# Loads split between GpSimd and SyncE, turns by DMA, and fixed orders in an attention and max-out kernel

## Chip, cores and metric

One core of a Trainium2 chip. The time is the device time of one execution in microseconds (us), measured over several runs; lower is better. Engines: TensorE (PE; its weight loads are PEld), VectorE (DVE), ScalarE (ACT), GpSimd (POOL), and SyncE (SP), which only issues transfers here. Transfers run on 16 DMA engines.

## What is computed

Attention over 4 batches, 8 heads, 768 positions and 64 channels, in which each query sees the keys less than 16 positions away and one summary (max for k, mean for v) per block of 32 positions; then a feed-forward stage over all 3072 rows of 512 channels.

```
k_sum = k.reshape(B, H, nb, 32, D).max(axis=3);  v_sum = v.reshape(B, H, nb, 32, D).mean(axis=3)
scores_l = scale * q @ k.T          (kept where |i - j| < 16)
scores_s = scale * q @ k_sum.T + log(32)
a = softmax(concat[scores_l, scores_s]);  x = a @ concat[v, v_sum]
g = maximum(x @ w1, x @ w2);  out = g @ w_out
```

All inputs and the output are float32; the matmuls run in bfloat16.

## The kernel before

The second stage is rewritten: with wd = w2 - w1, out = x (w1 w_out) + relu(x wd) w_out. The product w1 w_out (called w1o) is computed once.

Names in the plan: the first digit of a tag is the batch (0 to 3), the second the pair of heads (0 to 3), the third the group of queries (0 or 1: half of the positions, in three tiles of 128 rows). Loads: k and q per pair (k02 is batch 0, pair 2), v per half of the heads (v00, v01), a0 to a3 and b0 to b3 (quarters of w1 and w2), o0 to o3 (of w_out).

Per pair, `prep` casts k and q to bfloat16, turns each on PE by six 128x128 transposes (line 422), copies them from PSUM in the order of positions ("place"), takes the block maxima on DVE ("max"), copies the 32 neighbours of each tile of 64 positions ("halo") and the 24 block maxima into every tile ("sums"), so that one key tile holds 96 keys and the summaries. `scores` does 26 small matmuls per group (line 478), each on 64 rows for one head, then the exponential on ACT (line 485). In batch 0 the window is applied on PE by adding a tile of large negative numbers (line 470); in later batches by a multiplication on DVE or GpSimd (line 490). `values` does 12 matmuls per group (line 507) against a v that `place_v` has spread over tiles of 64 positions, with the block means (line 379) copied into each tile; DVE then divides (lines 518, 520) to x. After two pairs x is turned on PE by six transposes (line 536) and copied to xt.

`make_w12` makes wd and a bfloat16 w1, turns w1 on PE (line 573); `make_w1o` multiplies (line 594). `maxout` per batch and group: eight "hidden" tiles of four matmuls of 384 columns (line 607) with a relu each (line 612), then three "out" tiles, each in three parts of four matmuls of 512 columns: x w1o first (line 624), then two halves of g w_out (line 631); a copy and a store follow. Each part can stand apart in PE's order.

All loads and stores are issued by SP. 40 groups of four matmuls on the identity (line 666, "warm") occupy PE while it has nothing else. The order of each engine's work comes from a planner in the kernel: each step has a duration, dependences and a priority number, and whenever an engine is free in the planner's account the step with the best priority that can run is put next in that engine's program. The buffers (rings of tiles: six for float32 k and q, two for float32 v, eight banks of PSUM) are handed out in the same pass. On the chip each engine runs its program in that order and waits at the head of it.

Of the kernel before, what the change touches and what calls it, by code (L numbers as in the profile page):

```python
# [14 lines left out]
F32 = mybir.dt.float32  # L15
# [7 lines left out]
C = dict(  # L23
    first='k2 v0 k1 k0 q1 q0 b0 k3 q3 a0 v1 b2 b3 q2 a1 o0 a3 a2 o1 o2 b1 o3',
    later='q2 q0 k1 k3 k2 q3 q1 k0 v0 v1',
    b0=dict(v=84, vcast=('POOL ACT', 'ACT DVE'), vevac=('DVE', 'ACT'), pair=83,
             scores=(-128, 370), values=(-484, 84),
             kcast=('DVE POOL ACT', 'DVE POOL', 'ACT', 'DVE POOL ACT'),
             qcast=('DVE ACT', 'ACT', 'ACT POOL', 'POOL DVE'),
             kplace=('ACT', 'ACT', 'DVE ACT', 'DVE ACT'), qplace='ACT DVE',  # L30
             halo=('DVE POOL', 'DVE POOL', 'DVE POOL', 'POOL'),
             sums=('DVE POOL', 'DVE POOL', 'ACT', 'ACT'), mask='PE',
             xt=('DVE', 'DVE', 'DVE', 'ACT DVE')),
    b=dict(v=-315, vcast=('ACT DVE', 'ACT'), vevac='ACT', pair=95, scores=(43, 18),
             values=(-92, -34), kcast=('DVE POOL ACT', 'POOL', 'DVE POOL', 'DVE POOL'),
             qcast=('ACT POOL', 'DVE POOL ACT', 'DVE POOL ACT', 'POOL DVE'),
             kplace=('ACT', 'ACT', 'DVE', 'DVE'), qplace=('ACT', 'DVE', 'ACT', 'ACT DVE'),
             halo=('DVE ACT POOL', 'DVE ACT POOL', 'DVE ACT POOL', 'DVE ACT'),
             sums=('POOL', 'DVE', 'DVE POOL', 'POOL'), mask='DVE POOL', xt='DVE'),
    w12=2240, w1t=-1070, wo=1060, w1o=-830, moe=1300, wd='POOL',  # L40
    w1b=('ACT', 'POOL ACT', 'POOL ACT', 'POOL DVE'),
    wocast=('POOL DVE', 'POOL DVE', 'POOL DVE', 'DVE'), w1tcopy='ACT DVE', w1ocopy='ACT DVE',
    relu='ACT', outcopy='ACT', caps=dict(kq=5, sc=6, av=6, mm=7, x=3, warm=1), hold=2, warm=40,
    xdma=(), kqdma=(), tdma=1.5, hide=5.5, amean=8.5)
# [52 lines left out]
class Plan:  # L97
# [4 lines left out]

    LAG = {"PE": 0.25, "ACT": 0.2, "DVE": 0.15, "POOL": 0.2, "SP": 0.1}
    LAND, DEPTH, TURN = 2.2, 8, 0.08

    def __init__(self):
        self.tasks = []

    def op(self, engine, us, fn, read=(), write=(), change=(), touch=(), behind=(), prio=0.0, label="",
           mode="", port=False, dma=0.0, fill=False):  # L110
        t = Task()
        t.choice = isinstance(us, dict)
        t.us = us if t.choice else {engine: us}
        t.fn, t.label, t.mode, t.port, t.dma, t.fill = fn, label, mode, port, dma, fill
        t.prio = (prio, len(self.tasks))
        t.new, t.behind = [*write, *change], behind
        t.deps = {w for b in (*read, *change) for w in b.writers}
        for b in t.new:
            b.writers.append(t)
        for b in (*read, *touch, *t.new):  # L120
            b.users.append(t)
        self.tasks.append(t)
        return t
# [9 lines left out]

    def run(self):
        follow, left = {t: [] for t in self.tasks}, {}
        for t in self.tasks:
            left[t] = len(t.deps) + len(t.behind)
            for d in (*t.deps, *t.behind):
                follow[d].append(t)
        waiting = {e: [] for e in self.LAG}  # L140
        events = [0.0]

        def offer(t):
            t.at = max((d.done + self.LAG["SP" if d.dma else d.engine] for d in t.deps), default=0.0)
            heapq.heappush(events, t.at)
            for e in t.us:
                bisect.insort(waiting[e], t, key=lambda t: t.prio)

        for t in self.tasks:
            if not left[t]:  # L150
                offer(t)
        busy = dict.fromkeys(self.LAG, 0.0)
        landed = [0.0] * self.DEPTH
        order, mode = [], ""
        while len(order) < len(self.tasks):
            now = heapq.heappop(events)
            for e, queue in waiting.items():
                if busy[e] > now:
                    continue
                able = [t for t in queue if t.at <= now and not (t.dma and landed[-self.DEPTH] > now)]  # L160
                if e == "PE":
                    many = {m: sum(t.mode == m for t in able) > 1 for m in ("rows", "cols")}
                    able.sort(key=lambda t: t.fill or (t.mode != mode if mode else (
                        t.mode != "" and not many[t.mode] and now < t.at + C["hold"])))
                t = next((t for t in able if self.slots(t, now)), None)
                if t is None:
                    continue
                t.start, t.engine, us = now, e, t.us[e]
                if t.dma:
                    busy[e] = now + t.dma  # L170
                    t.done = max(landed[-1], now + self.LAND) + us
                    landed.append(t.done)
# [4 lines left out]
                elif e == "DVE" and t.port:  # L177
                    busy[e] = t.done = max(now, busy["POOL"]) + us
# [3 lines left out]
                for other in t.us:  # L182
# [540 lines left out]
```

## Time and profile before

| | |
|---|---|
| median of 3 runs | 181.82 us (179.27 to 182.73) |
| the profiled execution | 180.56 us, its span 178.9 us |
| granted TensorE clock | 0.995 |
| HBM read, written | 25.17 MB, 6.29 MB |

The busy share of an engine is an average over the whole span; the rows of single stretches tell which stage is limited by what. "Idle before" is the time an engine stood before a group, with what ended it. A row of the chain of waits names the work, or the transfer, that ended last at that point. DMA share can be over 1, since packets on one engine overlap. A few matmul records can be missing from a trace.

### The profile page before, as it was taken

Reading aid. Unit: us, or ns where it says so; the run is one execution under the profiler, and the core shown is the slowest. Engines: PE = TensorE matmul, PEld = TensorE weight load, DVE = VectorE, ACT = ScalarE, POOL = GpSimd, SP = SyncE. Lnnn points to the kernel's source line nnn. Section 1 sums busy time; section 2 is a strip of 40 time slices with the busy share of each in tenths; the row PEclk is TensorE's granted clock in tenths of the full one; section 3 lists DMA queues with packets and bytes.
Section 4 is the critical chain, followed back from the end, with each engine's and each line's share of the span. In section 5 each row is a group of like instructions: output and inputs, shape, how many; then the busy total and the mean of one; then the engine's idle time right before and its main releaser. Section 6 shows DMA issues by size and latency. Waiting matters only on the chain.

```text
span 178.9 us, 4689 instructions
## 1 busy us (share of the span) xinstructions
PE 167.5 (94%) x1946; PEld 102.3 (57%) x1968; DVE 100.7 (56%) x193; ACT 115.0 (64%) x188; POOL 57.6 (32%) x74
## 2 busy tenths in 40 slices
PE   6999878999999999989999999999999999999991
PEld 6976745665544666557545664664565545654440
DVE  4294984879799679879935770396772201200000
ACT  3597987578886882498989541896828238471212
POOL 7123436938373550037677500324110000000000
PEclk9999999999999999999999999999999999999998
DMA  5999999999979999999811101210111013000333
GB/s 149 280 376 332 295 385 388 402 382 238 290 222 276 299 256 349 260 251 312 279 59 62 59 4 59 87 36 0 60 62 62 0 59 117 4 0 0 117 117 117
DMA packets 42261, 31.76 MB, mean 178 GB/s; under 512 B 25856, under 2 KB 38144, under 8 KB 42240
## 3 DMA queue, kind: packets, MB, share of 16 engines
q1 hardware_dynamic: 42240, 31.46, 59.3%
q8 instruction: 15, 0.25, 0.6%
q14 instruction: 6, 0.05, 0.1%
HBM read 25.17 MB, written 6.29 MB: 176 GB/s over the span
## 4 chain that ended last, share of the span: by engine, by line
PE 70%; DMA 15%; issue 5%; DVE 4%; ACT 2%; SPq 1%; POOL 0%; POOLq 0%; DVEq 0%; ACTq 0%
PE banks L607 24%; PE banks L631 17%; PE banks L624 10%; DMA kqf<-in_q_dram 5%; DMA wf<-in_moe_w_out_dram 5%; DMA vf<-in_v_dram 4%; PE banks L478 3%; PE banks L507 3%; PE banks L422 3%; PE banks L594 3%; PE banks L666 3%; DVE kqb L277 2%; PE banks L536 2%; ACT vx L277 1%; PE banks L379 1%
## 5 line engine op out<-in xcount | busy, mean ns | idle before, releaser
L607 PE MATMUL banks<-xt,wd 128*128 128x384 bf16 x256 | 45.8, 327 | 0.0
L631 PE MATMUL banks<-wo,g 128*128 128x512 bf16 x181 | 44.7, 380 | 1.1 <-issue 0.8
L612 ACT ACTIVATE g<-banks 128x384 bf16<-128x384 f32 x64 | 31.3, 492 | 11.3 <-PE banks L607 10.8
L277 ACT COPY o<-banks 128x512 f32<-128x512 f32 x24 | 14.1, 585 | 31.8 <-PE banks L631 31.6
L607 PEld LDWEIGHTS <-wd 128*128 128x128 bf16 x256 | 23.6, 98 | 14.6
L485 ACT ACTIVATE pb<-banks,bias 128x768 bf16<-128x768 f32 x32 | 28.0, 900 | 3.4 <-PE banks L478 2.6
L631 PEld LDWEIGHTS <-g 128*128 128x128 bf16 x192 | 17.4, 98 | 18.2
L490 POOL TENSOR_TENSOR pb<-pb,mask 128x768 bf16<-128x768 bf16 x12 | 20.1, 1680 | 14.1 <-ACT pb L485 14.1
L624 PE MATMUL banks<-w1o,xt 128*128 128x512 bf16 x88 | 23.1, 380 | 0.5 <-issue 0.2
L277 DVE COPY vx<-vx 64x1584 bf16<-64x1584 bf16 (+3 forms) x32 | 19.8, 633 | 3.1 <-ACT vx L277 2.4
L422 PE MATMUL banks<-identity,kqb 128*128 128x128 bf16 x192 | 15.4, 220 | 2.3 <-DVE kqb L277 1.0
L277 POOL CAST kqb<-kqf 128x768 bf16<-128x768 f32 x11 | 10.5, 964 | 21.0 <-PE banks L422 12.7
L440 DVE TENSOR_REDUCE ks<-kx 128x24 bf16<-128x768 bf16 x16 | 14.8, 944 | 3.9 <-ACT kx L277 3.8
L520 DVE TENSOR_TENSOR xs<-banks,inv 128x384 bf16<-128x384 f32 x32 | 16.7, 546 | 0.3
L277 POOL COPY kx<-kx 128x32 bf16<-128x32 bf16 (+1 forms) x21 | 7.9, 409 | 26.5 <-ACT kx L277 25.1
L422 PEld LDWEIGHTS <-kqb 128*128 128x128 bf16 x192 | 12.0, 98 | 6.1 <-DVE kqb L277 1.5
L624 PEld LDWEIGHTS <-xt 128*128 128x128 bf16 x96 | 9.2, 98 | 10.2
L518 DVE RECIPROCAL inv<-banks 128x6 f32<-128x6 f32 x32 | 5.4, 186 | 16.9 <-PE banks L507 16.8
L666 PE MATMUL banks<-identity 128*128 128x128 bf16 x160 | 13.0, 247 | 1.4 <-POOL identity masks.py:199 1.4
L277 DVE CAST kqb<-kqf 128x768 bf16<-128x768 f32 x10 | 7.7, 781 | 10.8 <-issue 7.1
L277 ACT CAST kqb<-kqf 128x768 bf16<-128x768 f32 x11 | 9.1, 832 | 5.7 <-DMA kqf<-in_k_dram 3.6
L666 PEld LDWEIGHTS <-identity 128*128 128x128 bf16 x160 | 11.6, 113 | 1.5 <-POOL identity masks.py:199 1.4
(60 smaller groups left out, 176.0 us busy)
## 6 DMA issues: line engine op xcount, KB each, us to landing
kqf<-in_k_dram SPq DMA_DIRECT2D x16, 384.0 KB, 5.7
vf<-in_v_dram SPq DMA_DIRECT2D x8, 768.0 KB, 8.1
kqf<-in_q_dram SPq DMA_DIRECT2D x16, 384.0 KB, 7.0
out_dram<-o SPq DMA_DIRECT2D x20, 256.0 KB, 2.0
wf<-in_moe_w_dram SPq DMA_DIRECT2D x8, 512.0 KB, 8.3
wf<-in_moe_w_out_dram SPq DMA_DIRECT2D x4, 512.0 KB, 9.0
out_dram<-o SPq DMA_DIRECT2D x4, 224.0 KB, 2.3
out_dram<-o SPq DMA_DIRECT2D x4, 32.0 KB, 2.1
```

What stands on the lines that cost most here:

```text
L277: {"DVE": nc.vector.tensor_copy, "ACT": nc.scalar.copy, "POOL": nc.gpsimd.tensor_copy}[engine](out=o, in_=i)
L422: nc.tensor.transpose(out=bank(ps, S, BF16)[:, 128 * j:128 * j + 128], in_=src.ap[:, j].rearrange("p h d -> p (h d)"), identity=identity[:])
L440: op("DVE", 0.95, lambda: nc.vector.tensor_reduce(out=ks.ap[:].rearrange("p (t s) -> p t s", s=2), in_=kx[b, hp].ap[:, :, 0:64].rearrange( ...
L485: op("ACT", 0.91, lambda: nc.scalar.activation(out=pb.ap[:].rearrange("p a t q -> p a (t q)"), in_=view(), func=ACT.Exp, bias=bias[:], sca ...
L490: nc.gpsimd if e == "POOL" else nc.vector).tensor_tensor(
L518: op("DVE", 0.19, lambda: nc.vector.reciprocal(out=inv.ap[:], in_=av()[:, :, :, D:D + 1]), read=[ps], write=[inv], prio=prio, label=f"inv ...
L520: op("DVE", 0.55, lambda: nc.vector.tensor_tensor(out=x.ap[:, hp % 2], in0=av()[:, :, :, 0:D], in1=inv.ap[:].to_broadcast([128, GU, 2, D]) ...
L607: nc.tensor.matmul(out=bank(ps, GT), lhsT=wd[n // 2].ap[:, c, 128 * (n % 2):128 * (n % 2) + 128], rhs=x.ap[:, c, :], start=(c == 0), stop= ...
L612: nc.scalar.activation(out=g.ap[:, n, :], in_=bank(ps, GT), func=ACT.Relu)
L624: nc.tensor.matmul(out=bank(ps), lhsT=x.ap[:, c, sl], rhs=w1o[c].ap[:], start=(c == 0), stop=False)
L631: nc.tensor.matmul(out=bank(ps), lhsT=g.ap[:, f, sl], rhs=wo[f // 2].ap[:, f % 2, :], start=False, stop=(f == FC - 1))
L666: nc.tensor.matmul(out=bank(ps, 128), lhsT=identity[:], rhs=identity[:], start=True, stop=True)
```

## The change

1. All planned priorities go. Each engine's order is a list of names written out (`ORDER`), SP's and GpSimd's with the loads and turns in them; the planner only hands out buffers along it and settles nothing of the order. PSUM's shares per kind are new.
2. Loads: SP keeps 13 at the start (k00, k02, q01, q03, v00 and the eight quarters of w1 and w2), as float32. All others are issued by GpSimd and cast to bfloat16 on the way, k and q into eight new buffers, v into its place, w_out into its own tile; their casts on the engines go. K and q of batch 3 are loaded by head, in pieces of 64 channels.
3. Turns: x of batches 1 to 3 (12 turns) and k and q of batch 3 (8) by DMA from SP instead of on PE. K and q of batches 0 to 2 are turned on PE in twelve matmuls of half width, each head to its half of the partitions.
4. Batch 0: k is kept as one row of positions with 32 more at the end, and no summaries are copied into tiles. The block maxima stand in one tile `kp`; `scores` adds their product by two to four matmuls per group over up to 384 columns; `values` adds the block means by a second set of 12 matmuls with `vm`.
5. v is laid out by parity of the tile, and its spreading copies follow that layout.

```
+X_BY_DMA, KQ_BY_DMA = (1, 2, 3), (3,)
+KEEP_TYPE = "k00 k02 q03 q01 v00".split()
+CAPS = dict(kq=5, sc=2, av=3, mm=3, out=3, x=5, warm=7)
+WARM = 40
+ORDER = dict(
+    PE="""warm, warm, warm, warm, warm, warm, warm, warm, warm, warm, warm, warm, warm, warm, warm, warm, turn
+        k02, warm, warm, turn q01, warm, warm, warm, warm, warm, warm, warm, warm, warm, warm, warm, warm,
+        warm, warm, warm, turn q03, warm, warm, warm, turn w1 0, warm, warm, warm, warm, turn q02, means 00,
+        scores 021, scores 020, turn w1 3, turn k01, turn w1 2, turn k03, scores 011, scores 010, turn q00,
+        values 011, turn k00, values 010, turn w1 1, scores 031, means 01, scores 030, scores 001, scores
+        000, w1o 10, w1o 30, w1o 00, values 001, values 000, values 030, turn k13, values 020, turn x011,
...
+        values 230, out 102 b, out 100 b, out 102 c, out 112, out 100 c, out 112 b, out 101, out 112 c, out
+        101 b, scores 330, scores 331, out 101 c, hidden 203, hidden 207, scores 320, scores 301, hidden
...
+        out 212, scores 300, scores 321, out 201 b, hidden 214, out 201 c, out 200 b, out 212 b, values 300,
+        values 321, out 212 c, out 200 c, out 210, out 211, out 210 b, out 211 b, out 210 c, out 211 c,
+        hidden 300, hidden 303, out 300, out 301, out 311, hidden 315, hidden 317, hidden 314, hidden 310,
...
+    ACT="""cast k02, cast q01, place k02, w1t 0, place q02, means 001, means 000, exp 021, exp 020, w1b 2,
+        place k01, halo k01, place k03, exp 011, exp 010, place k00, w1t 1, exp 031, means 011, means 010,
...
+    DVE="""zeros 3, zeros p0, zeros p1, zeros 0, zeros 2, zeros 1, spread hide, mask, place q01, halo k02, max
+        k02, cast q03, place q03, spread v001, spread v002, spread v000, w1b 3, wd 3, w1t 3, w1t 2, max k01,
...
+    POOL="""identity, zeros vm, amean, load q02, hide, load k01, load k03, load q00, ones 0, load v01, w1b 0,
+        load wo0, load wo2, load k13, ones 1, cast v00, load wo1, wd 0, load q12, load q10, load k11, cast
+        k00, halo k00, load q13, wd 2, load wo3, load k12, load v10, load q11, load k10, load v11, load v20,
...
+    SP="""load k02, load q01, load b3, load q03, load a0, load v00, load b1, load a3, load b0, load a2, load
+        a1, load k00, load b2, turn x131, store 001, store 000, turn q33, turn x110, turn x111, store 002,
...
+        t = queue[0]
+        if self.ready(t) > now or (t.dma and landed[e][-self.DEPTH] > now) or not self.slots(t, now):
             continue
...
-    kqf = Ring(tiles("kqf", 6, [128, 2, J * D], F32))
+    kqf = Ring(tiles("kqf", 3, [128, 2, J * D], F32))
+    kqc = Ring(tiles("kqc", 8, [128, 2, J, D], BF16))
...
+    op("POOL" if cast else "SP", 1.08, lambda: (nc.gpsimd if cast else nc.sync).dma_start(
+        out=f.ap[:].rearrange("p h j d -> p h (j d)") if cast else f.ap[:],
+        in_=(k, q)[n][b, 2 * hp:2 * hp + 2].rearrange("h (p j) d -> p h (j d)", j=J)),
...
+    for j in range(J):
+        for h in range(2):
+            nc.tensor.transpose(out=bank(ps, S, BF16)[64 * h:64 * h + 64, 128 * j:128 * j + 128],
+                                in_=src.ap[:, h, j], identity=identity[:])
...
+    for n0, n1, at in queries(GN * grp, GN) if b == 0 else ():
+        for a in range(2):
+            r = slice(64 * a, 64 * a + 64)
+            nc.tensor.matmul(out=view()[:, a, n0:n1], lhsT=kp[hp].ap[r],
+                             rhs=qx[b, hp].ap[r, at:at + n1 - n0], start=False, stop=(n1 == GT))
...
+    if b:
+        nc.tensor.matmul(out=o, lhsT=p, rhs=tile_v, start=True, stop=True)
+    else:
+        nc.tensor.matmul(out=o, lhsT=p[0:96], rhs=tile_v[0:96], start=True, stop=False)
+        nc.tensor.matmul(out=o, lhsT=p, rhs=vm[:, 2 * hp + a, 0:D + 1], start=False, stop=True)
...
-    if b in C["xdma"]:
+    if b in X_BY_DMA:
         op("SP", 1.0, lambda: nc.sync.dma_start_transpose(
             out=x_t.ap[:, hp - 1:hp + 1, :].rearrange("p h (u n) -> p (h u) n", n=128),
             in_=x.ap[:].rearrange("p h u a d -> p (h u a d)")),
...
+    cast = f"o{n}" not in KEEP_TYPE
+    f = wfs[n, 2] = wo[n] if cast else Buf(wfr)
```

More of the change, by code (lines that the diff above doesn't have):

```diff
@@ L19 @@
 ACT = mybir.ActivationFunctionType
[L23 to L44, printed above, removed]
@@ L181, in run @@
                     busy[e] = t.done = now + us
[L182 to L190 removed]
+                    pool = t.done if e == "POOL" else pool
+                order.append(queue.pop(0))
+                for at in (now, busy[e], t.done, t.done + 0.15, *(self.ready(q[0]) for q in queues.values() if q)):
+                    heapq.heappush(events, at + 1e-9)
         for t in order:
```

478 lines of the change are left out of this document (271 added, 207 removed).

## The prediction, made before the result was known

> **What bounds the kernel now.** I read the page's first two parts, then the busy time by stretch, then the chain of waits, then the start in order of time.
>
> ```profile
> PE 167.5 (94%) x1946; PEld 102.3 (57%) x1968; DVE 100.7 (56%) x193; ACT 115.0 (64%) x188; POOL 57.6 (32%) x74
> ...
> DMA  5999999999979999999811101210111013000333
> ```
>
> TensorE is the busy engine; the transfers are dense for the first half and thin after it. Busy time by stretch tells two stages apart (columns: stretch, its length, then busy time and count for PE, weight loads, DVE, ACT, POOL, then clock, DMA share, GB/s). The second fence is the same view for line 666 alone, the warm-up matmuls (PE, weight loads, clock, DMA share, GB/s):
>
> ```profile
> 0.00:35.00 35.00, 30.49 (x508) 23.84 (x510) 22.89 (x52) 25.51 (x32) 16.71 (x30) 1.00 1.04 324
> 35.00:175.00 140.00, 136.97 (x1441) 78.42 (x1459) 77.85 (x142) 88.88 (x157) 40.89 (x45) 1.00 0.50 142
> 175.00:178.90 3.90, 0.00 (x0) 0.00 (x0) 0.00 (x0) 0.57 (x1) 0.00 (x0) 0.77 0.38 134
> ```
> ```profile
> 0.00:35.00 35.00, 12.97 (x160) 11.59 (x160) 1.00 1.04 324
> ```
>
> From 35 to 175 us PE is full (3 us open in 140). Before that it has 30.49 us busy, of which 12.97 is warm-up that computes nothing: 17.5 us of useful work in 35, while the DMA share is 1.04. So the end is set by when the loads let PE begin in earnest, plus the work that PE then has, plus 3.9 us for the last copy and store. The chain of waits (start, length, what) says the same:
>
> ```profile
> 8.28 9.49 DMA kqf<-in_q_dram
> ...
> 22.89 9.35 DMA wf<-in_moe_w_out_dram
> 32.26 0.92 DVE wo L277
> ...
> 35.11 0.34 PE banks L536 x6
> 35.44 0.34 PE banks L422 x6
> ...
> 36.45 1.73 PE banks L594 x8
> ...
> 60.11 0.50 PE banks L507 x24
> ...
> 144.38 0.86 PE banks L624 x4
> ...
> 174.99 0.58 ACT o L277
> ```
>
> Two loads carry it up to 32.24 us, and then almost only PE. The rows also give prices on the path: six transposes of a 128x128 tile take 0.34 us, 24 values matmuls (two groups of scores) 0.50, one third of an output tile 0.86. The useful PE work of the kernel is 17.5 + 140 = 157.5 us, with the 3 open us counted in. The profiled run took 180.56 us for a span of 178.9, so 1.7 lies outside; the median of the runs, 181.82, is 1.3 above it. My sum is for the profiled run.
>
> **The change, part by part.** First PE's own work. X of batches 1 to 3 is no longer turned on PE: 12 turns of 0.34 = 4.1 us less. K and q of batch 3: 8 x 0.34 = 2.7 less. K and q of batches 0 to 2 are turned in twelve half-width matmuls for six full ones; they write two different halves of the output columns' partitions, and line 507's matmuls, which alternate between halves in the same way, go at 0.50/24 = 0.02 us each, so I count no change (bounds: nothing gained, up to 0.34 more per turn if the halves do not overlap, 24 turns, 8 us; the L507 row is the nearest and speaks for the low end). Batch 0 gains work: each scores group gets a product of the block maxima over 384 columns per head. Its nearest rows are the hiding matmuls of the same width, in order of time on PE:
>
> ```profile
> 14.23 0.49 PE L470 MATMUL banks<-hide,identity 128*128 128x384 bf16 x2
> 14.65 0.35 PE L478 MATMUL banks<-qx,kx 64*128 64x64 bf16 x12
> 14.93 0.50 PE L470 MATMUL banks<-hide,identity 128*128 128x384 bf16 x2
> ```
>
> Two of them cost 0.42 us start to start, the whole group 0.70. The new pair reads 64 rows each, on different rows, as line 478's do, and its twelve go by in 0.28; so 0.21 if the two run side by side, 0.42 if not. I take 0.21: 8 x 0.21 = 1.7 us (up to 3.4). Values of batch 0 double from 12 to 24 matmuls: 8 x 0.25 = 2.0 us (up to 4.0). Net: -4.1 - 2.7 + 1.7 + 2.0 = -3.1 us, hence 154.4 us of useful work (between 153.5, with a little gained in switching, and 158).
>
> Second, when PE begins in earnest. The new order of PE is a list, and PE waits at its head. It runs all 40 groups of warm-up, then turns, one weight turn after another and the first four scores; its gate is "turn k00". That load is the twelfth of SP's 13: k02, q01, b3, q03, a0, v00, b1, a3, b0, a2, a1 come before it. Ahead of that gate stand only 7 turns (2.4 us), 3 weight turns of eight (1.4), a mean of twelve like a values group (0.25), 4 scores of 0.91 (3.6) and a values group (0.5): 8.1 us useful. Everything else, 154.4 - 8.1 = 146.3 us, comes after it. What the loads cost, from the casts on ScalarE that wait for them:
>
> ```profile
> 4.22 0.83 ACT L277 CAST kqb<-kqf 128x768 bf16<-128x768 f32 x1 [2.13 <-DMA kqf<-in_k_dram]
> ...
> 7.75 1.47 ACT L277 CAST vx<-vf 128x1536 bf16<-128x1536 f32 x1
> ...
> 20.76 1.48 ACT L277 CAST vx<-vf 128x1536 bf16<-128x1536 f32 x1
> ...
> 30.95 1.04 ACT L277 CAST w1b<-wf 128x1024 bf16<-128x1024 f32 x1 [0.32 <-DMA wf<-in_moe_w_dram]
> 33.25 0.83 ACT L277 CAST kqb<-kqf 128x768 bf16<-128x768 f32 x1 [1.26 <-DMA kqf<-in_q_dram]
> 34.24 0.83 ACT L277 CAST kqb<-kqf 128x768 bf16<-128x768 f32 x1 [0.15 <-DMA kqf<-in_q_dram]
> ```
>
> The first k is there at 4.2 us. One q follows another by 1.0 us. Between the weight tile at 30.95 and the w_out tile that lands at 32.24 (chain) lies 1.3. A half of v takes 3.5 after the first k (7.75), 3.0 after the q that landed at 17.77 (20.76); I take 3.25. A casting load writes half the bytes but reads the same; no row shows one, so its price lies between half and the whole of the plain one, or above it by what GpSimd takes to write its list; I take the whole, 1.0. Then k00 lands at 4.2 + 3 x 1.0 (q01, q03, itself) + 7 x 1.3 + 3.25 = 19.55, if GpSimd's transfers cost it nothing, and 4.0 later, at 23.55, if the four that PE needs before that point (q02, k01, k03, q00) go in between. Its cast is on GpSimd:
>
> ```profile
> L277 POOL CAST kqb<-kqf 128x768 bf16<-128x768 f32 x11 | 10.5, 964 | 21.0 <-PE banks L422 12.7 <-PE banks L573 4.9 <-DMA kqf<-in_k_dram 3.5
> ...
> L563 POOL TENSOR_TENSOR wd<-wf,wf 128x1024 bf16<-128x1024 f32 x4 | 10.3, 2598 | 4.2 <-DMA wf<-in_moe_w_dram 4.2
> ```
>
> 1.0 us, behind "wd 0" (2.6) and three load issues in GpSimd's list, which wait for b0, three loads (3.6 us) earlier; that just hides them, and would cost up to 2 us if an issue takes 1 us. So PE goes on at 24.6 us: 24.6 + 146.3 = 170.9, + 3.9 = 174.8 of span, + 1.7 = 176.5 us.
>
> The casts that go (28 of the 32 of k and q, seven of v's eight, w_out's four) and the six spread-out sums and means of batch 0 lie on DVE, ACT and POOL, which are 56%, 64% and 32% busy and not on the path after 35 us: no gain there. Before 35 us they shorten each step by a cast (0.83) but it is the landing that gates. The warm-up costs nothing while PE waits anyway; it hides under 24.6 us.
>
> Third, the moved queues. SP's list holds only turns and stores after its 13 loads, so a turn waits behind stores, and those wait for their copies; behind a waiting mask or halo on GpSimd wait loads of later batches, for which the eight new buffers give a lead. The turns matter by their slack: the last x of batch 2's first group follows "values 230", and the first reader, "hidden 203", stands ten output thirds later, 8.6 us; in batch 3 it is eight thirds, 6.9 us, less the 0.7 us that DVE needs to make x. What a turn by DMA takes no row shows. The nearest ones, to landing:
>
> ```profile
> vf<-in_v_dram SPq DMA_DIRECT2D x8, 768.0 KB, 8.1
> ...
> out_dram<-o SPq DMA_DIRECT2D x20, 256.0 KB, 2.0
> ```
>
> A turn moves 192 KB, less than a store, mostly when the DMA is thin: between 2.0 and 8.1 us, nearer the store. So it stays under the slack. The Trainium skill speaks against it: "VectorE: DVE Perf Modes", The three transpose paths, gives 1309 ns for a 128x128 tile by DMA and 390 ns on TensorE, by which six tiles one after another would be some 7.9 us by an estimate; no run here shows it, and the sum would become some 178 us.
>
> **The rivals.** *GpSimd's transfers go first (slower).* If the two queues share the DMA engines instead of going in the order of issue, SP's tiles wait for whatever GpSimd has issued: besides the four also v01 (3.25), wo0, wo2, wo1 (3.9) and k13 (1.0), 8.15 us. PE then stands at "turn w1 2" and "turn k00", with scores ready behind them. 176.5 + 8.15 = 184.6 us; from 5.3 us of such transfers on the kernel is slower than before. For it: the DMA share is already 1.04, and all five stand in GpSimd's list early. Against it: wo0 and what follows wait behind "w1b 0", thus for a0's landing. By the Trainium skill's "DMA: Bandwidth & Descriptors", Queues, rings and completion order, each engine takes the queues in turn, packet by packet, which is this rival; the rows here, with one load queue, neither bear it out nor deny it.
>
> *Cast loads are cheaper.* If the halved writing sets the price, four loads cost 0.5 each, 2.0 us less, and v00, whose rate is lower (768 KB in 3.25 against 384 in 1.0), goes beside the other queue at 2.0, 1.25 less: 176.5 - 3.25 = 173.2 us.
>
> *Turns land late.* With 11 us to landing, 3 us over the slack, once a batch: 9 us more, 185.5 us. Against it: the DMA is thin by then:
>
> ```profile
> 90.00:178.00 88.00, 83.47 (x798) 46.50 (x808) 30.23 (x65) 47.39 (x83) 15.90 (x15) 0.99 0.15 55
> ```
>
> **How the numbers follow.** Forecast 0.42, cheaper casts 0.22, GpSimd first 0.20, late turns 0.08; 0.08 for a list whose head waits at places I did not price. A measurement here can tell about 2%: below 178.2 us is faster, above 185.5 slower. The forecast's own range is 174.5 to 179.5 (PE work from -1 to +3): 0.33 faster, 0.09 the same. Cheaper casts: 0.22 faster. GpSimd first runs from 182 to 187: 0.12 the same, 0.08 slower. Late turns slower; the rest 0.03 the same, 0.05 slower. Together 0.55, 0.24, 0.21. The range from 171.5 (cheaper casts with 1.7 off) to 185.5 leaves out less than 2 in 10.
>
> **What would show it.** Right: "turn k00" on PE near 24.6 us, little idle after it, useful work near 154 us, L536 with 24 matmuls for 96, first matmul of line "hidden" before 40 us. The rival is right if PE's longest wait is for a weight tile's cast or for k00 near 33 us, while v01 and w_out have long landed. Cheaper casts: q02's successors land 0.5 us apart. Late turns: PE waits for a DMA into xt after 90 us. I would be wrong altogether if PE's work grew, by transposes of half width at 0.68 a turn.

## The result, and the profile after

| | before | after |
|---|---|---|
| median | 182.27 us (179.27 to 183.11, 4 runs) | 193.22 us (192.19 to 198.02, 4 runs) |
| the profiled execution, its span | 180.56, 178.9 | 193.74, 192.0 |
| granted clock | 0.995 | 0.947 |

The ratio is 1.0683, 95% interval 1.0476 to 1.0889: slower, where 176.5 us was forecast. The ratio leaves out runs more than 1.5% above the fastest of their kernel (182.73 and 183.11 before, 198.02 after). The page of the changed kernel, first two parts:

```profile
PE 168.0 (87%) x2090; PEld 99.5 (52%) x2112; DVE 106.6 (56%) x206; ACT 85.2 (44%) x143; POOL 77.0 (40%) x98
...
PE   7983083699999999997999799999999999999991
...
PEclk9999555589999999999999999999999999999999
DMA  5999999744999961899999999699320346200404
```

A slice is 4.8 us. PE stands for most of the fourth, fifth and seventh slice, and its clock is halved from the fifth to the eighth. Busy time by stretch, cut where "turn k00" stands (41 us):

```profile
0.00:35.00 35.00, 19.92 (x284) 16.36 (x284) 8.50 (x23) 8.53 (x11) 15.75 (x30) 0.77 1.14 244
35.00:41.00 6.00, 5.57 (x94) 3.47 (x96) 4.24 (x5) 3.65 (x6) 3.19 (x5) 0.61 0.77 134
41.00:188.00 147.00, 142.40 (x1724) 79.70 (x1738) 93.85 (x178) 72.40 (x127) 58.05 (x64) 1.00 0.90 111
```

From 41 to 188 us lie 147.0 us, and 146.3 were forecast for the work behind that gate; the gate itself was forecast at 24.6. PE in order of time shows it, the number in brackets being the wait and what ended it:

```profile
23.91 0.85 PE L448 MATMUL banks<-vx,amean 128*64 128x128 bf16 x12 [8.00 <-POOL vx L332]
...
31.16 1.04 PE L676 MATMUL banks<-identity,w1b 128*128 128x128 bf16 x8 [2.96 <-DVE w1b L332]
...
35.43 1.04 PE L676 MATMUL banks<-identity,w1b 128*128 128x128 bf16 x8 [2.45 <-ACT w1b L332]
...
40.98 0.50 PE L498 MATMUL banks<-identity,kqb 128*64 128x128 bf16 x12
```

PE waits 8.00 us at "means 00" for the cast of v00, then 2.96 and 2.45 us for w1's fourth and third quarters ("turn w1 3" and "turn w1 2", the loads a3 and a2), and reaches "turn k00" (line 498) at 40.98, 16.4 us later than forecast. It never waits for k00 itself: from a2's turn on it works without a pause through 5.5 us of its list, at a mean clock of 0.61. The chain of waits tells why these tiles are late:

```profile
4.67 12.68 SPq L652
17.39 1.20 SPq L652
18.64 1.12 SPq L652
19.81 14.50 DMA wf<-in_moe_w_dram
34.33 1.05 ACT w1b L332
35.43 1.04 PE banks L676 x8
```

SyncE needs 12.68 us to issue b1, which stands behind v00 in its list, and a2, issued at 19.81, takes 14.50 us to land. K00 landed at 36.8 us, not 23.55. The last columns of the view by stretch (clock, DMA share, GB/s) show the transfers meanwhile, first the changed kernel, then the kernel before:

```profile
16.00:20.00 4.00, 0.00 (x0) 0.00 (x0) 0.00 (x0) 0.76 (x1) 0.25 (x1) 0.90 1.72 159
20.00:24.00 4.00, 0.09 (x3) 0.09 (x4) 0.10 (x1) 0.00 (x0) 1.60 (x2) 0.50 1.33 224
24.00:38.00 14.00, 8.59 (x92) 5.01 (x93) 5.14 (x9) 4.98 (x8) 5.65 (x6) 0.50 1.00 279
```
```profile
16.00:20.00 4.00, 3.59 (x88) 2.68 (x88) 2.21 (x4) 4.00 (x6) 2.98 (x3) 1.00 1.23 243
20.00:25.00 5.00, 4.61 (x95) 3.54 (x92) 4.57 (x12) 4.92 (x8) 0.15 (x1) 1.00 1.07 367
```

While v00 (SyncE) and v01 (GpSimd) are both under way, from 16 us to their landings at 22.3 and 23.7, the DMA share is up to 1.72 and the rates are 159 and 224 GB/s. These count what is written, and a casting load writes half of what it reads: from 16 to 24 us GpSimd's queue wrote 0.84 MB and SyncE's 0.68, so that some 295 GB/s were read. In the kernel before, one half of v, nearly by itself, ran at 243 (16 to 20 us) and other tiles at 367. So the two halves together were read no slower than one was there; there were two of them. Then SyncE's tiles and w_out, k13 land by turns: wo0 25.9, b1 26.9, wo2 28.0, k13 29.9, a3 30.4, wo1 32.1, b0 32.8, a2 34.3, a1 35.8, k00 36.8.

For the whole I count **useful work**: each PE matmul but the warm-up at its full-clock price, 0.216 us for 512 columns (four of line 727 take 0.86 in the chain), in proportion for others but not under 0.054, half for those on half the rows or columns. Matmuls whose records are missing from a trace are in the totals and not in the counts by time. The kernel before has 153.3 us of it, the changed one 150.8.

| useful work done by | 40 us | 60 us | 100 us | last matmul |
|---|---|---|---|---|
| before | 21.7 | 40.0 | 77.4 | 174.5 us |
| after | 7.0 | 26.4 | 61.9 | 187.8 us |

The last matmul comes 13.3 us later: 13.6 us behind at 60 us, less 2.5 us of work saved, and 2.2 more lost after 60 us (127.8 us for 124.4 of work; before, 114.5 for 113.3). So in this kernel the loss is made in the start, and afterwards it is not won back; whether its rest would be as fast behind an early start is another question, asked further below.

### The profile page after: what moved, and what is told of

Read it like the earlier page. It is cut to its first block, busy times and chain, and to the rows that moved or that the text cites. A ratio compares the mean times of both kernels' runs of the same rounds, so it can differ in the third digit from the quotient of the medians.

```text
span 192.0 us, 4925 instructions
## 1 busy us (share of the span) xinstructions
PE 168.0 (87%) x2090; PEld 99.5 (52%) x2112; DVE 106.6 (56%) x206; ACT 85.2 (44%) x143; POOL 77.0 (40%) x98
## 4 chain that ended last, share of the span: by engine, by line
PE 67%; SPq 10%; DVE 9%; DMA 8%; issue 2%; ACT 2%; ACTq 0%
PE banks L734 22%; PE banks L710 17%; PE banks L727 9%; SPq L652 8%; DMA wf<-in_moe_w_dram 8%; DVE vx L332 5%; PE banks L498 4%; PE banks L572 4%; PE banks L697 3%; PE banks L608 3%; PE banks L565 2%; DVE pb L588 1%; DVE g L717 1%; PE banks L448 1%; DVE ks L530 1%
## 5 line engine op out<-in xcount | busy, mean ns | idle before, releaser
L710 PEld LDWEIGHTS <-wd 128*128 128x128 bf16 x256 | 24.3, 98 | 18.3 <-issue 0.7
L715 ACT ACTIVATE g<-banks 128x384 bf16<-128x384 f32 x43 | 21.1, 491 | 28.3 <-PE banks L710 28.0
L332 DVE COPY vx<-vx 32x1320 bf16<-32x1320 bf16 (+3 forms) x36 | 24.1, 691 | 11.0 <-POOL vx L332 10.4
L588 POOL TENSOR_TENSOR pb<-pb,mask 128x768 bf16<-128x768 bf16 x10 | 16.4, 1640 | 20.3 <-ACT pb L583 20.3
L332 ACT COPY o<-banks 128x512 f32<-128x512 f32 x16 | 9.4, 585 | 22.2 <-PE banks L734 22.1
L717 DVE TENSOR_SCALAR g<-banks 128x384 bf16<-128x384 f32 x21 | 11.5, 556 | 12.3 <-PE banks L710 11.9
L621 DVE RECIPROCAL inv<-banks 128x6 f32<-128x6 f32 x32 | 5.9, 189 | 12.3 <-PE banks L608 9.4
L498 PE MATMUL banks<-identity,kqc 128*64 128x128 bf16 x240 | 10.6, 230 | 1.5 <-issue 1.5
L448 PE MATMUL banks<-vx,amean 128*64 128x128 bf16 x96 | 4.5, 232 | 8.4 <-POOL vx L332 8.0
L332 DVE COPY o<-banks 128x512 f32<-128x512 f32 x8 | 5.5, 682 | 9.6 <-ACT o L332 6.0
L588 DVE TENSOR_TENSOR pb<-pb,mask 128x768 bf16<-128x768 bf16 x14 | 9.1, 655 | 2.4 <-ACT pb L583 2.3
L498 PEld LDWEIGHTS <-kqc 128*64 128x64 bf16 x240 | 7.9, 115 | 4.1 <-issue 3.8
## 6 DMA issues: line engine op xcount, KB each, us to landing
kqc<-in_q_dram POOLq DMA_DIRECT2D x10, 192.0 KB, 4.8
kqc<-in_k_dram POOLq DMA_DIRECT2D x10, 192.0 KB, 5.8
wo<-in_moe_w_out_dram POOLq DMA_DIRECT2D x4, 256.0 KB, 10.2
```

What stands on the lines that cost most here:

```text
L332: {"DVE": nc.vector.tensor_copy, "ACT": nc.scalar.copy, "POOL": nc.gpsimd.tensor_copy}[engine](out=o, in_=i)
L498: nc.tensor.transpose(out=bank(ps, S, BF16)[64 * h:64 * h + 64, 128 * j:128 * j + 128], in_=src.ap[:, h, j], identity=identity[:])
L588: nc.gpsimd if e == "POOL" else nc.vector).tensor_tensor(
L710: nc.tensor.matmul(out=bank(ps, GT), lhsT=wd[n // 2].ap[:, c, 128 * (n % 2):128 * (n % 2) + 128], rhs=x.ap[:, c, :], start=(c == 0), stop= ...
L715: nc.scalar.activation(out=g.ap[:, n, :], in_=bank(ps, GT), func=ACT.Relu)
L717: nc.vector.tensor_scalar_max(g.ap[:, n, :], bank(ps, GT), 0.0)
```

## The experiments

Theory S: SyncE's tiles that PE's list asks for wait for GpSimd's transfers. Theory L: it is the list on PE, which puts the late tiles too far ahead. Theory G: it is GpSimd's list, in which later loads stand behind waiting work. Theory R: v00's many small pieces hold SyncE's own issue, whatever GpSimd sends. Ratios are to the kernel before, run on the same chip, with 95% intervals; the changed kernel has 1.068.

**Which transfers hold SyncE's.** w_out and k13 moved behind k00's cast in GpSimd's list:

```
-load wo0, load wo2, load k13, ones 1, cast v00, load wo1, wd 0, ..., cast k00, halo k00
+ones 1, cast v00, wd 0, ..., cast k00, load wo0, load wo2, load k13, load wo1, halo k00
```

> Changed kernel with four GpSimd loads (three of w_out's quarters, one k of batch 1) moved behind the cast of k00 in GpSimd's list; nothing else. Theory S (the two load queues share the DMA engines): SP's last tiles come earlier by what those four took between them, 4.9 us by the prices of the prediction: k00 lands near 32 us instead of 36.8, PE goes on with turn k00 near 36 instead of 41, time about 188 to 190 us. Theory R (SP's own issue is held up by v00's many small pieces, whatever GpSimd sends): k00 still lands near 37, time within 1 us of the changed kernel's 193.

Measured: 189.45 us, 1.0446 (1.0347 to 1.0545). K00 landed at 31.0, 5.8 us earlier, useful work at 60 us rose from 26.4 to 30.9. In the chain of waits a2 now takes 9.47 us instead of 14.50, and a half-width turn (line 507 here) 0.34, as long as a full one before:

```profile
19.09 9.47 DMA wf<-in_moe_w_dram
...
43.41 0.34 PE banks L507 x12
```

S holds: k00 came earlier by about what the four moved transfers take (4.9 us by the prices), and the ratio fell by 0.024, some 4 us. Six other profiles with these loads unmoved have k00 between 34.9 and 37.7 us. R falls as the cause of k00's delay, for SyncE's issue of b1 was held as long as before (12.62 us). The same with v01 moved too ("load v01" in front of the four):

> As the run before, and v01 moved there as well. Theory S: 8.15 us or more off the landing of k00 (near 27 to 28 us), turn k00 near 31, but v01 now lands about 4 us after it and holds the means of v01, so that the time is 183 to 187 us. Theory R: k00 still near 36, time 192 to 195 us.

Measured: 189.92, 1.0477 (1.0374 to 1.0579): k00 at 27.8, a further 3.2 us earlier (v01 had been priced at 3.25), with SyncE's issue still held for 12.55 us, and no gain in time, where 183 to 187 was expected. The waits of PE (us in total, times, longest) tell where it went:

```profile
PE banks L457 <- POOL vx L341: 4.7, 1, 4.7
PE banks L457 <- DMA vx<-in_v_dram: 3.1, 1, 3.1
```

v01 lands at 36.5 now, and the means wait for it. Then v00 taken from SyncE's list and loaded with a cast by GpSimd:

```
-KEEP_TYPE = "k00 k02 q03 q01 v00".split()
+KEEP_TYPE = "k00 k02 q03 q01".split()
```

> Changed kernel with v00 loaded by GpSimd with a cast, ahead of v01, instead of by SP as float32; its cast on GpSimd goes. Theory R: SP's issue is no longer held from 4.7 to 17.4 us, its weight tiles land from 12 us on and k00 before 28; time 184 to 188 us. Theory S: the sum of bytes ahead of k00 is the same, but v00 now competes only at half the rate: k00 lands 3 to 5 us earlier (32 to 34), v00 itself later; time 189 to 194 us.

Measured: 193.19, 1.0666 (1.0565 to 1.0767). The longest hold of SyncE's issue is 5.7 us now and k00 lands at 25.5. That is earlier than S had it (32 to 34) and inside R's bound (28). But with both halves of v in the other queue most of their bytes now come after k00: v00 lands only at 28.2, v01 at 30.7, and the time is S's (189 to 194):

```profile
PE banks L457 <- DMA vx<-in_v_dram: 13.7, 1, 13.7
```

One tile's lead is another's delay. The first 38 us carry the same bytes however they are split (8.9 MB written in the changed kernel, 8.8 to 9.0 in these three runs); what counts is which tile is last for the head of PE's list.

**The halved clock.** 58 more warm-up groups put into PE's list where it waits:

> Changed kernel with 58 more groups of warm-up matmuls on PE, put where it waits (36 ahead of the means of v00, 10 and 12 ahead of the two weight turns); loads untouched. Theory C (the clock, which fell to half while PE stood idle, costs what PE does between 24 and 41 us): the clock stays at 1.0, the stretch from the last weight tile's cast (35.4 us) to turn k00 shrinks from 5.5 to about 3 us, time 190 to 191.5 us. If only the landings count, turn k00 is not earlier than 1 us before 41 and the time stays at 193.

Measured: 192.05, 1.0627 (1.0527 to 1.0728), granted clock 0.99 to 1.00. In the profiled execution, the fastest of the five (189.72), "turn k00" comes at 37.9 us, 3.1 earlier; but a2 landed 2.0 us earlier there too, with the loads untouched, and from a2's turn to "turn k00" PE took 4.3 us instead of 5.5. The clock costs a microsecond or so, within the interval; the waits are the loss.

**PE's list, and GpSimd's.** The loads left as they are, and PE, ACT and DVE given the work of batch 0 in the order in which its tiles land:

```
-means 00, scores 021, scores 020, turn w1 3, turn k01, turn w1 2, turn k03, ..., turn k00
+scores 021, scores 020, turn k01, scores 011, scores 010, turn k03, ..., means 00, ..., turn w1 2, turn k00
```

> Changed kernel with every load where it was; only the lists of PE, ACT and DVE up to the last values of batch 0 are rearranged, so that scores, values and x of pairs 1, 2 and 3 stand ahead of the weight turns 3, 2, 1 and of k00. Theory L (work that is ready stands behind a head that waits for a late load): about 13.5 us useful are done when k00 is turned near 38 us, instead of 8.1 at 41; time 183 to 186 us. Theory B (the landings alone, k00 and the weight tiles at 34 to 37 us, set the start): turn k00 near 38 to 39 us and what follows is no shorter; time 190 to 193 us.

Measured: 193.94, 1.0706 (1.063 to 1.0782): nothing. By 40 us 13.2 us of useful work were done (7.0 in the changed kernel), by 60 us 26.7 (26.4). L falls as the whole cause. GpSimd's list could be the next hold, since w_out's fourth tile landed at 53.8 in this run:

```
-cast k00, halo k00, load q13, wd 2, load wo3, load k12
+cast k00, load q13, load wo3, load k12, halo k00, wd 2
```

> The lists of the engine-orders run, and in GpSimd's list the loads of q13, w_out's fourth tile and k12 moved from behind halo k00 and wd 2 to directly behind cast k00. Theory G (with PE's list mended, the start is held by GpSimd's in-order list, whose loads stand behind halo k00 and wd 2): w_out's fourth tile lands near 43 us (there 53.8), the first hidden matmul starts at 50 to 53 us (there 59.1), time 185 to 189 us (there 193.9). Rival S alone (only the landing of k00 and of SP's last weight tiles sets the time, and that is as before): first hidden near 58 to 59 us, time 192 to 194.5.

> The changed kernel with the same edit of GpSimd's list alone (q13, w_out's fourth tile and k12 directly behind cast k00). Theory G: PE is held until 41 us by k00 anyway, but what comes after it no longer waits for GpSimd: first hidden at 54 to 57 us (changed kernel 58.8), time 189 to 191.5 us. Rival S alone: first hidden 58 to 59, time 192 to 194.

> Both causes taken away at once: w_out's tiles 0, 2, 1 and k13 behind cast k00, as in the run with w_out later, then q12, q10, k11, q13, w_out's fourth and k12 with only halo k00 between them and wd 0, wd 2 behind; PE, ACT and DVE by the lists of the engine-orders run. S and G together: k00 lands at 28 to 31 us, first hidden at 48 to 52 us, time 182 to 187 us. S alone: what the run with w_out later gave, 188 to 190. If the start is held by something else again (the casts and turns of w_in on DVE and ACT): first hidden later than 54 and 189 or more.

Measured: 192.93, 1.0587 (1.0507 to 1.0667); 194.69, 1.067 (1.0565 to 1.0775); 199.36, 1.0923 (1.0826 to 1.102). In the first, w_out's fourth tile landed at 44.8 as expected, and the first hidden matmul still started at 59.9, in the second at 60.5: G falls as the cause of the loss, though the first ratio (1.059 against 1.071 for the lists alone) leaves room for some 2 us. In the third, the edit itself set a new hold: q12, q10 and k11 stood behind "halo k00", whose k comes late by these lists, were issued at 46.8 us and landed from 50.4 on. A run with the lists, SyncE's order and the place of w_out in GpSimd's list all changed was no better:

> The same kind of rearrangement with the loads rearranged too: SP k02, q01, q03, a0, k00, v00, then a3, a2, a1, b3, b0, b1, b2; GpSimd's w_out and first k of batch 1 behind the cast of v00. All 16 turns and scores of batch 0 need only k and q, which should land by about 15 us; v00 and v01 by 22 us; the weight tiles from 23 us on. Theory L with sharing: PE has some 17 us of useful work done at 31 us, 4 us earlier than the kernel before, and 3 us less work in all: time 173 to 177 us. If the PE work of the change is not smaller, 176 to 180. If the landings in batch 1 hold it, 180 or more.

Measured: 191.74 us, the four runs (187.38 to 193.77) too far apart for a ratio; 173 to 177 was expected. K00 landed at 13.1, v00 at 22.2; 14.9 us of useful work by 40 us, 29.1 by 60.

**What the DMA turns are worth.** In the changed kernel, x of batches 1 to 3 back on PE, with its twelve copies on DVE. The first version put the turns too early, and PE waited 9.9 us for x:

> Changed kernel with x of batches 1 to 3 turned on PE and copied by DVE again (12 turns of six transposes, 12 copies of 0.55 us); the start is untouched. If the turns by DMA were worth their PE time and no more, the time rises by up to 4.1 us to 195 to 197.5 us. If PE waits for the turns by DMA somewhere, it rises less or falls below 193.

Measured: 210.37, 1.1613 (1.1525 to 1.1701); it says nothing of the price of a turn. The second puts each turn where x is ready:

```
-X_BY_DMA, KQ_BY_DMA = (1, 2, 3), (3,)
+X_BY_DMA, KQ_BY_DMA = (), (3,)
```

> The changed kernel with x of batches 1 to 3 turned on PE again (xs -> identity matmuls and a copy to xt, as batch 0 still is), each turn put where its x is ready in PE's list; the loads and all of the start are the changed kernel's. If the DMA turns save PE time as predicted (4.1 us of PE work for x and q, k of batch 3, of which x is some 4 us and nothing of it is lost elsewhere): 195 to 197.5 us. If they save nothing (PE had that time free anyway): 192.5 to 194.5. If DMA turns cost (late, or in the way of other transfers): below 192.

Measured: 198.20, 1.09 (1.0814 to 1.0986), 4.0 us above the changed kernel by the ratios (0.0217 x 182.2), with 3.9 us more useful work. The two intervals overlap (1.081 to 1.099, 1.048 to 1.089), so the 4.0 has an error of about its own size. Then the reverse, in the kernel before, whose planner lays out the rest:

```
-xdma=(), kqdma=(), tdma=1.5
+xdma=(1, 2, 3), kqdma=(3,), tdma=1.5
```

> The kernel before with one part of the change alone: x of batches 1 to 3 and k, q of batch 3 turned by DMA (its planner lays out the rest; loads, casts and block sums as before). If the turns are worth the PE work they take away (predicted 4.1 for x and 2.7 for k, q): 175 to 178.5 against 182.2. If only x's 4 us count, since k and q of batch 3 still need a cast on an engine and another DMA: 178 to 180. If the DMA turns stand in SyncE's in-order list and hold loads and stores behind them: 182 to 186.

> The kernel before with x of batches 1 to 3 turned by DMA, and k, q of batch 3 turned on PE as before. If the gain of the run of the kernel before with all DMA turns (179.9 against 182.0) comes from x: the same, 179.5 to 180.5. If k, q of batch 3 bring half of it or more: 181 or more. If they cost (their DMA and their load in pieces of 256 bytes): below 179.5.

Measured: 179.86, 0.987 (0.9815 to 0.9925), and with x alone 179.22, 0.9881 (0.9823 to 0.9939). Both are faster than the kernel before by 1.2 to 1.3%, some 2.2 us, which is clear of the intervals though under 2%. The intervals do not tell the one from the other: x brings it, and k and q of batch 3 add nothing that can be seen. The page of the first of the two, part 6 (count, median us from issue to landing):

```profile
xt<-xs SPq DMA_TRANSPOSE x12, 3.9
```

**The start laid out anew.** Same loads on each queue, but batch 0's first; all lists and the banks for each kind of work laid out for that:

```
-SP="""load k02, load q01, load b3, load q03, load a0, load v00, load b1, load a3, load b0, load a2, load a1, load k00
+SP="""load k02, load v00, load k00, load q01, load a0, load b0, load q03, load a1, load b1, load a3, load b3, load a2
-CAPS = dict(kq=5, sc=2, av=3, mm=3, out=3, x=5, warm=7)
+CAPS = dict(kq=5, sc=3, av=3, mm=6, out=3, x=3, warm=2)
```

> The changed kernel with the same loads on each queue, but what batch 0 needs first in both: SyncE k02, v00, k00, q01, a0, b0, q03 and then the rest of w_in; GpSimd q02, q00, k01, k03, v01, w_out; the lists of all engines and the banks for each kind of work are laid out anew for these loads, and hidden no longer stands behind all of the products of w_out with w_in. Theory S (what holds the start is that the tiles which PE's list asks for first are the last of a shared queue): k00 lands by 12 to 15 us, v00 by 18, useful PE work of 20 or more by 40 us (changed kernel 7.0, kernel before 21.7), first hidden at 33 to 40 us, time 178 to 184. If the loss is not in the start: 190 or more.

In two more, batch 0's k, q and v are loaded by SyncE alone, as float32:

```
-KEEP_TYPE = "k00 k02 q03 q01 v00".split()
+KEEP_TYPE = "k00 k01 k02 k03 q00 q01 q02 q03 v00 v01".split()
```

> Batch 0's k, q and v all loaded by SyncE as fp32 and cast on the engines, as in the kernel before; GpSimd's queue starts with w_out's tile 0 behind its cast for w_in's tile 0, so that the two queues do not share the DMA engines in the first 15 to 20 us; all else of the change stays (cast loads from there on, x of batches 1 to 3 and k, q of batch 3 turned by DMA, block sums apart); lists laid out anew. Theory S: k00 lands by 9 us, v00 by 8, as in the kernel before; useful PE work at 40 us 21 to 26, first hidden 30 to 36, time 177 to 181: at or under the kernel before (182.2). If sharing costs nothing by itself and only order counts: the same as the run with the start rearranged on the same split. If the loss is not in the start: 190 or more.

> As the run with batch 0 by SyncE, with v01 behind all k and q of batch 0 and w_in's first tile, and GpSimd's list beginning with k13, q12, q10 in place of w_out: SyncE's order k02, v00, k01, k00, q00, q01, q02, k03, q03, a0, v01. Theory S: within 2 us of the run with batch 0 by SyncE (178 to 182), since v01 is wanted only from means 01 on.

And the new starts up to 42 us in front of the changed kernel's own order:

> The start of the run with the start rearranged on the same split (its lists up to about 42 us), and behind it every list in the changed kernel's own order. In that run 36.7 us of useful PE work were done by 60 us (changed kernel 26.4, kernel before 40.0), but its rearranged middle lost 7 us again between 60 and 100 us with DVE busy 4.9 of 5. Theory S (all of the loss is in the start, and the rest of the changed kernel is as fast as forecast): useful work by 60 us 34 to 38, by 100 us 70 to 74 (changed kernel 61.9), time 181.5 to 186. If the changed kernel's rest only looked fast because it was fed late, and slows down with an early start (DVE, DMA): 187 or more.

> The same with batch 0's k, q and v by SyncE alone: the start of the run with v01 late (182.8), then the changed kernel's own order. Theory S: 179 to 183. If its rest slows down with an early start: 184 or more.

| | k00 lands | useful by 40 | by 60 | by 100 us | median | ratio (interval) |
|---|---|---|---|---|---|---|
| before | 9.8 | 21.7 | 40.0 | 77.4 | 182.0 | 1 |
| after | 36.8 | 7.0 | 26.4 | 61.9 | 193.2 | 1.068 (1.048 to 1.089) |
| start anew, same split | 9.7 | 19.0 | 36.7 | 65.4 | 190.1 | 1.041 (1.033 to 1.049) |
| batch 0 by SyncE | 8.9 | 19.7 | 37.0 | 65.9 | 189.1 | 1.037 (1.030 to 1.044) |
| the same, v01 late | 10.1 | 20.3 | 37.8 | 72.1 | 182.8 | 1.006 (1.001 to 1.010) |
| new start, old rest | 10.3 | 18.3 | 30.6 | 60.9 | 192.5 | 1.060 (1.051 to 1.069) |
| batch 0 by SyncE, old rest | 10.1 | 19.8 | 35.3 | 68.3 | 186.6 | 1.029 (1.022 to 1.037) |

The starts came out nearly as S expects, with 18 to 20 us of useful work by 40 us instead of 7, and on the split queues as well as by SyncE alone: with the right tiles first, the split start and SyncE's differ by a microsecond (their lists differ too). By these two it is the order of the tiles that counts, and sharing costs little by itself. The times did not follow. "Start anew", expected at 178 to 184 us, came out at 190.1, the time that I had given to a loss outside the start. Only one of the five reaches the kernel before, and two layouts with batch 0 by SyncE, expected within 2 us of each other, lie 6 us apart. They differ in the place of v01, in GpSimd's first loads and in every list, so which of these decides is not shown. "New start, old rest" made a stall of its own at 49 to 52 us, and the execution that was profiled took 2 us more than its median; what its rest can do stays open. The last row is the nearest to a test of the start alone: it wins back 0.039 of the 0.068, some 7 us of 12. The other 5 us are lost behind the start, for the same rest runs slower with an early start than in the changed kernel: 33.0 us of work between 60 and 100 us, against 35.5.

What may limit it there is read from the stretch 60 to 100 us (PE, weight loads, DVE, ACT, POOL): the kernel before, the changed kernel, "start anew" and "v01 late", in this order, each with its first 40 us.

```profile
0.00:40.00 40.00, 35.49 (x563) 27.50 (x566) 26.58 (x58) 29.06 (x38) 18.45 (x33) 1.00 1.05 332
...
60.00:100.00 40.00, 38.62 (x556) 23.55 (x562) 31.17 (x63) 30.11 (x50) 21.03 (x22) 1.00 0.83 227
```
```profile
0.00:40.00 40.00, 24.49 (x340) 19.02 (x340) 11.99 (x27) 11.53 (x15) 18.94 (x34) 0.74 1.10 231
...
60.00:100.00 40.00, 37.37 (x537) 21.47 (x542) 34.42 (x61) 24.89 (x47) 27.03 (x30) 1.00 1.21 116
```
```profile
0.00:40.00 40.00, 35.22 (x659) 26.88 (x661) 21.78 (x48) 20.33 (x28) 21.64 (x39) 0.91 1.18 242
...
60.00:100.00 40.00, 33.38 (x497) 18.41 (x502) 36.25 (x60) 22.57 (x39) 24.79 (x25) 0.96 1.17 112
```
```profile
0.00:40.00 40.00, 33.89 (x678) 26.29 (x679) 23.45 (x51) 24.59 (x33) 18.35 (x35) 1.00 0.99 252
...
60.00:100.00 40.00, 36.51 (x575) 20.68 (x580) 34.23 (x67) 25.48 (x44) 28.36 (x28) 1.00 1.29 134
```

DVE is busy 34 to 36 of 40 us in the three versions of the changed kernel, 31 in the kernel before. The change took 30 us of casts and copies off ACT (115.0 to 85.2 in all) and put 6 us on DVE (100.7 to 106.6: 21 relus and 8 output copies are new there). When the start is late DVE has done 12.0 us of work by 40 us instead of 26.6, and from 60 us on it has hardly any room to catch up. PE's waits from 60 to 100 us bear this out in part only. Those that DVE ended come to 2.9 of 6.6 us in "start anew", 4.5 of 6.7 in batch 0 by SyncE, 1.2 of 3.5 with v01 late, 2.7 of 5.9 and 1.9 of 4.9 in the two with the old rest; the others were ended by ACT or show no wait for another engine, and in "start anew" 1.1 us was for a turn of x by DMA. No run moves DVE's work to ACT, so DVE as the limit of that stretch is read from the traces and not shown.

## Why the prediction was wrong

**What failed is the gate at 24.6 us**, and in it the term "k00 lands at 23.55": SyncE's twelve transfers one after another plus only the four of GpSimd's that PE needs before that point, as if the transfers went in an order by need. They took 36.8 - 23.55 = 13.2 us more, and "turn k00" came 16.4 us late. A2, whose cast ended PE's last wait before it, stands two places ahead of k00 in the same list and was late with it (34.3 us); the other 3 us are list work that PE still had ahead of "turn k00", at the lower clock. The mechanism is the rival "GpSimd's transfers go first", to which I gave 0.20, and the trace of before could not show it. Its sign was "PE's longest wait is for a weight tile's cast or for k00 near 33 us, while v01 and w_out have long landed". Roughly so: the longest wait is for v00's cast (8.0), which I did not name, then come the weight tiles' (3.0 and 2.5), and v01 landed at 23.7, w_out's first three by 32.1. Its price was about right, 8.15 us for five transfers: with these five moved away k00 landed 9.0 us earlier (27.8). Its sum, 184.6 us, was too low all the same, since 27.8 is still 4.2 us after 23.55. Of these some 2.5 us are lost early: a0 landed at 12.3 in that run, where the prices give 8.8, or 9.8 with q02 ahead of it. It landed at 9.9 with v00 out of SyncE's list, but also at 10.0 and 10.2 in two profiles with v00 in it, so the cause of this part stays open. And the objection that wo0 and its followers wait for "w1b 0" was weak: a0 landed at 12.8.

By the Trainium skill's "DMA: Bandwidth & Descriptors", Issuing engines are not separate DMA queues, transfers started by different engines run on the same 16 DMA engines and interleave. The trace agrees (SyncE's and GpSimd's landings alternate from 24 to 33 us), and the prediction should have started from it: the last tile of a long list is then late by what the other list moves meanwhile.

**PE's own work, right within a microsecond.** -3.1 us forecast, -2.5 counted. In order of time, one batch 0 scores group of the changed kernel at full clock:

```profile
43.73 0.50 PE L565 MATMUL banks<-hide,identity 128*128 128x384 bf16 x2
44.16 0.46 PE L572 MATMUL banks<-qx,kn 64*96 64x64 bf16 x12
44.45 0.33 PE L578 MATMUL banks<-qx,kp 64*128 64x384 bf16 x2
44.71 0.50 PE L565 MATMUL banks<-hide,identity 128*128 128x384 bf16 x2
```

A group takes 0.98 us start to start where it took 0.70, of which line 578's pair is 0.26: forecast 0.21, so the two run nearly side by side. A group of values costs 0.40, not 0.50. The half-width turn costs nothing (0.34 for twelve). The turns of x by DMA are worth some 4.0 us in the changed kernel, with the wide error given above; 4.1 were forecast. Of k and q of batch 3 I counted 2.7 us; in the kernel before they bring nothing beside x (0.987 against 0.988), and x itself 2.2 there.

**"146.3 us of work after the gate"** fitted the result (147.0) partly by luck. In the five runs with an early start PE did 28.7 to 34.3 us of useful work between 60 and 100 us, against 35.5 in the changed kernel and 37.4 in the kernel before: with the gate at 24.6 us the forecast time would probably not have come out either. A likely reason in part is DVE, which I had dismissed (56% busy, not on the path after 35 us) by its share over the whole span. The range has a slip as well: PE work from -1 to +3 us about 176.5 gives 175.5 to 179.5, not 174.5.

**The other rivals.** Cheaper casts: GpSimd's first loads landed 1.3 to 1.5 us apart, and later ones, alone, 1.0 (k11 after q10), not 0.5, so the rival falls. Late turns: PE never waits for a DMA into xt in the changed kernel; the view of that tile gives its landings:

```profile
DMA to landing us min/median/max: 2.8/3.5/8.2
```

Under the slack of 8.6 and 6.9 us but for the longest, and there PE had other work. The 7.9 us worked out from the Trainium skill's "VectorE: DVE Perf Modes", The three transpose paths, is near the longest (8.2), not the usual price: six tiles by DMA take 3.5 us at the median here.

## What to carry to other kernels

A second load queue gave no second set of DMA engines here. Before loads are split, write out the landing of each tile with the other queue's transfers added at their full price (8.15 us by the prices, 9.0 measured), and put first, in both, what the consumers' fixed lists ask for first. When an engine's list stalls at its head, see which other engine stood idle with it, and whether that one has room later: DVE was busy 34 of 40 us here. And a change of many parts is worth taking apart: one of them, x turned by DMA, made the kernel before 1.2% faster by itself.

## What the hardware showed unexpectedly

**A copy on DVE can last as long as GpSimd's instruction.** In the changed kernel, DVE and then GpSimd in order of time, the spread of the summaries at 102.57 us:

```profile
102.57 3.46 DVE L332 COPY vx<-vx 32x1320 bf16<-32x1320 bf16 x2
```
```profile
102.21 1.71 POOL L409 DMA_DIRECT2D kqc<-in_k_dram  x2
103.92 1.67 POOL L588 TENSOR_TENSOR pb<-pb,mask 128x768 bf16<-128x768 bf16 x1
```

The two copies take 3.46 us: the first 0.82 beside the load issues, the second 2.71 beside a multiplication on GpSimd, and it ends 0.4 us after that (105.6). Elsewhere such a copy takes 0.5 to 0.6. By shapes, the same kernel's spreading copies:

```profile
L332 DVE COPY vx<-vx 32x1320 bf16<-32x1320 bf16 x14 | 10.2, 732 | 10.7 <-POOL vx L332 10.4
L332 DVE COPY vx<-vx 64x1584 bf16<-64x1584 bf16 x8 | 6.4, 803 | 0.1
L332 DVE COPY vx<-vx 32x1584 bf16<-32x1584 bf16 x6 | 5.7, 951 | 0.0
```

The shortest of each shape take 0.49, 0.57 and 0.56 us, so that 28 copies take some 7.5 us of DVE's time above that (22.3 less 14 x 0.49, 8 x 0.57 and 6 x 0.56), in part in the very stretch in which DVE is full. In "new start, old rest" one small copy took 3.43 us instead of 0.23 beside GpSimd's "wd 2" and a load issue, and PE stood 3.1 us behind it. By the Trainium skill's "SBUF — State Buffer", SBUF: two separate sides, the pair of ports that DVE and GpSimd share is an exclusive lock held for the whole instruction; the trace agrees for GpSimd's arithmetic: four copies, begun at 44.3, 60.9, 71.1 and 103.3 us, all end 0.4 us after the GpSimd instruction beside them. For load issues on GpSimd, 0.7 to 0.9 us each for k and q, it is not clear: beside one of them alone such a copy took its shortest time (0.50 us at 92.3) or longer (0.89 instead of 0.57 at 90.8).

**The issue behind a transfer in small pieces can be held long.** Behind one load of v, in pieces of 256 bytes, the next issue on SyncE took 12.68 us, and 12.55 with v01 and w_out moved away; without v00 in the list the longest took 5.7. In the kernel before the longest such hold in the start was 7.98 us, behind v01. What of it is due to GpSimd's loads was not separated.
